# A fused state-space and feed-forward block with its gradients: channel order, one pass of magnitudes, split gates and a pipeline of state sums

## The chip, the cores and the metric

The kernel runs on one core of one Trainium2 chip. The metric is the device time of one execution in microseconds. A core has TensorE (PE, with its weight loads shown apart as PEld), VectorE (DVE), ScalarE (ACT), GpSimd (POOL) and SyncE (SP), and 16 DMA engines. Here nearly all transfers are issued by SP, in order.

## What is computed

For `x` of 2048 tokens by 512 channels the reference normalizes `x` to `xn`, runs a state-space convolution with 128 complex states per channel (`s`), runs a feed-forward net on the same `xn`, gates the one with the other, and returns the output and the gradients of all inputs but `B_x`, twelve arrays of bf16.

```python
P = jnp.exp(logdA[:, :, None] * l[None, None, :])
K = jnp.einsum("dn,dnl,dn->dl", Cc, P, dB).real
...
Yf = Uf * Kf[None, :, :, :]
y = irfft2(Yf, ...) + u * Dskip
...
h = silu(x @ w1);  out = h @ w2
...
xn = _layernorm(x); s = _A_ref(xn, ...); g = silu(_B_ref(xn, w1, w2))
return x + s * g
```

## The kernel before

The 512 channels are four blocks `b` of 128. Within a block a channel has two indexes, `q` (32) and `a` (4). The state-space part keeps its tables in the order (q, a); the channels of `xn`, `ds` and the outputs are in natural order, and strided access patterns lead from one to the other.

**Setup.** `layer_norm` (L223) makes `xn` from four chunks of `x`, `make_consts` (L108) the DFT matrices (`TF` by a sine on ACT, L142), `ssm_params` (L320) the rates `lamr` and `tau` and the weights `CT`.

**Forward.** `gen_ffn_fwd` (L481) is 8 chunks of 256 tokens: transposed `xn`, 56 matmuls a chunk with `W1` (L495), casts of `hT` on ACT, SiLU (L500), matmuls with `W2` (L507), stores to `Hd` and `Od`. Interleaved with it runs a chain over the blocks: `gen_tables` (L347) and `gen_conv_fwd` (L453). The tables need magnitudes `mag`, 31 exponentials of `lamr` (L356), and phases (sine, L376); their products are `E` and `Y`, stored to `Ed` and `Yd`; matmuls with `Y` (L408) and `SEL` (L419) give the convolution kernel, stored to `Kd`. `gen_conv_fwd` takes the spectrum `U` of `xn` and `KX` of the kernel (`dft_fwd`, L252, with a transposing DMA `dB` between two matmul stages), multiplies them (`cplx_mul`, L295), and goes back with `dft_inv` (L275), whose last matmuls (L291) write PSUM in natural channel order through a strided pattern.

**Gates.** For each block in turn `gen_gate_ds` (L515) loads the feed-forward result `Od` and the incoming gradient, makes `g` by SiLU and `ds`, stored to `dSd`; `gen_gate` (L529) loads `s` from `Sd` and `x`, writes the first output and `do`, the gradient that enters the feed-forward net. `g` has one buffer.

**Backward.** `gen_ffn_da` (L698) makes `dh` (L721, L723) and the gradient of `xn` (L732) for 8 chunks. Beside it a chain runs `gen_conv_bwd` (L547), which takes the spectrum of `ds` and gives the gradients of the kernel (`dKd`) and of `xn` (`dUd`), and `gen_ssm_bwd` (L585) for each block. That folds `dK` (L609), makes `Gb` (L615), and then works through four groups of 8 `q`: `YT` by transposing DMAs from `Yd`, matmuls `ps_v` (L628) that write PSUM in a strided order, casts `Vb` on ACT, four products `T` with `E` on DVE (L636), and sums over the 21 exponents, 84 matmuls of 64 columns with an identity (L641), all tiles with a single buffer. After four groups the block's parameter gradients follow (L655 on). What is left of the chain runs beside `gen_dw2` (L739), `gen_ln_bwd` (L772) and `gen_dw1` (L754).

**Order.** The generators are interleaved by weights, which gives the order in which the program is written; a scheduler then orders the instructions of each engine by that order and by when their operands are expected. On the chip each engine and each DMA queue keeps that order.

Of the kernel before, what the change touches and what calls it, by code (L numbers as in the profile page):

```python
# [9 lines left out]
ALU = mybir.AluOpType  # L10
# [5 lines left out]
P = 128  # L16
# [62 lines left out]

def interleave_until(gens, weights, other):  # L80
# [13 lines left out]
def slope_less_one(nc, u, h):  # L94

    nc.scalar.activation(out=h, in_=h, func=ACT.Tanh, scale=0.5)
    nc.vector.tensor_scalar(out=h, in0=h, scalar1=-0.5, scalar2=0.5, op0=ALU.mult, op1=ALU.add)
    nc.vector.tensor_single_scalar(out=u, in_=u, scalar=-1.0, op=ALU.add)
    nc.vector.tensor_tensor(out=u, in0=u, in1=h, op=ALU.mult)
# [8 lines left out]
def make_consts(k, wp):  # L108
# [141 lines left out]
def dft_fwd(k, U, X, ev):  # L252
# [22 lines left out]
def dft_inv(k, Y, ev, consume, natural=True):  # L275
    nc, w8, pc = k.nc, k.dft, k.pc
    A2 = w8.tile([P, 2, 16, P], BF16, name="dA2", tag="w8")
    for g0 in range(0, 16, 4):
# [5 lines left out]
        ev(A2[:].rearrange("p c t (g e) -> p g (c t) e", e=8)[:, g0:g0 + 4], ps[:])  # L284
    for h in range(2):
        ps = pc.tile([P, 8, P], F32, name="ps_i1", tag="pc")
        for j in range(8):
            t = 8 * h + j
            o = ps[:, j].rearrange("p (q a) -> p a q", a=4) if natural else ps[:, j]
            for c in range(2):  # L290
                nc.tensor.matmul(out=o, lhsT=k.TI[:, 2 * t + c, :], rhs=A2[:, c, t, :], start=(c == 0), stop=(c == 1))  # L291
# [3 lines left out]
def cplx_mul(k, out, a, b, conj=False):  # L295
# [24 lines left out]
def ssm_params(k, wp):  # L320
    nc, tbl, D = k.nc, k.p1, k.D
    TT = nc.vector.tensor_tensor
    S = load_params(k, wp, 0, D)
    ldt = wp.tile([P, D], BF16, name="ldt")
    nc.scalar.dma_start(ldt[:], k.ins["A_log_dt"].unsqueeze(0).to_broadcast([P, D]))
    nc.scalar.activation(out=k.dt[:], in_=ldt[:], func=ACT.Exp)
# [609 lines left out]
```

## Time and profile before

| | us |
|---|---|
| runs shown: median (lowest to highest) | 884.84 (877.52 to 887.74) |
| the profiled execution, its own time | 882.32 |
| its span, first to last instruction | 880.5 |
| mean granted TensorE clock | 0.901 |

The stages, by the first and last instructions of their parts: setup until about 48 us, forward to 309 (the last `ps_k` matmuls), the last block's transform and the gates to 419 (the first `ps_da` matmul), then the backward stages to the end. In the slices below (40 equal slices of the span) a digit is the busy share of an engine in tenths, PEclk the granted clock in tenths.

```profile
PE   0567697989968733602579999999999678878987
DVE  6967778569368500874385885977957456543420
ACT  0597978889888342432466847646752477632311
PEclk9989699999989675655889999999999899988999
DMA  8626367386556469697757569869545999757573
```

The row of PE has a trough in slices 14 to 19, which is the stretch from 309 to 419 us, and the clock falls with it.

### The profile page before, as it was taken

Reading aid. Unit: us, or ns where it says so; the run is one execution under the profiler, and the core shown is the slowest. Engines: PE = TensorE matmul, PEld = TensorE weight load, DVE = VectorE, ACT = ScalarE, POOL = GpSimd, SP = SyncE. Lnnn points to the kernel's source line nnn. Section 1 sums busy time; section 2 is a strip of 40 time slices with the busy share of each in tenths; the row PEclk is TensorE's granted clock in tenths of the full one; section 3 lists DMA queues with packets and bytes.
Section 4 is the critical chain, followed back from the end, with each engine's and each line's share of the span. In section 5 each row is a group of like instructions: output and inputs, shape, how many; then the busy total and the mean of one; then the engine's idle time right before and its main releaser. Section 6 shows DMA issues by size and latency. Waiting matters only on the chain. (4 is left out here: it accounts for less than half of the span.)

```text
span 880.5 us, 14322 instructions
## 1 busy us (share of the span) xinstructions
PE 652.9 (74%) x5692; PEld 464.6 (53%) x5692; DVE 542.5 (62%) x1141; ACT 510.4 (58%) x753; POOL 10.8 (1%) x70
## 2 busy tenths in 40 slices
PE   0567697989968733602579999999999678878987
PEld 0444364756636521401356787766876344447866
DVE  6967778569368500874385885977957456543420
ACT  0597978889888342432466847646752477632311
POOL 2000000000000000000000000000000000000000
PEclk9989699999989675655889999999999899988999
DMA  8626367386556469697757569869545999757573
GB/s 245 149 86 162 140 193 212 90 237 186 142 179 206 135 179 253 173 253 178 194 158 207 159 197 233 187 160 253 113 125 145 200 244 249 184 130 148 122 179 84
DMA packets 300151, 155.61 MB, mean 177 GB/s; under 512 B 215858, under 2 KB 286772, under 8 KB 297012
## 3 DMA queue, kind: packets, MB, share of 16 engines
q1 hardware_dynamic: 299796, 154.44, 68.3%
q8 instruction: 44, 0.72, 0.3%
q10 hardware_dynamic: 288, 0.26, 0.1%
q14 instruction: 23, 0.19, 0.1%
HBM read 48.23 MB, written 60.30 MB: 123 GB/s over the span
## 5 line engine op out<-in xcount | busy, mean ns | idle before, releaser
L495 PE MATMUL ps_h<-XT,W 128*128 128x256 bf16 x448 | 61.6, 285 | 38.1 <-DMA XT<-xn 28.4
L270 PE MATMUL ps_s<-dB,F 128*128 128x512 bf16 x96 | 40.4, 420 | 43.5 <-DMA dB<-dA 37.0
L495 PEld LDWEIGHTS <-W 128*128 128x128 bf16 x448 | 44.5, 103 | 49.8 <-issue 25.1
L636 DVE TENSOR_TENSOR T<-Vb,Eb 128x1344 bf16<-128x1344 bf16 x64 | 51.0, 852 | 30.3 <-ACT Vb L41 30.3
L41 ACT CAST Vb<-ps_v 128x672 bf16<-128x672 f32 x64 | 44.3, 719 | 40.1 <-PE ps_v L628 34.3
L41 ACT CAST dA<-ps_i 128x1024 bf16<-128x1024 f32 x48 | 46.6, 1018 | 34.7 <-PE ps_i L282 30.5
L260 PEld LDWEIGHTS <-TF 128*128 128x128 bf16 x384 | 37.4, 112 | 54.9 <-DMA ds_b<-dSd 36.5
L747 PE MATMUL ps_w<-do,a_tok 128*128 128x512 bf16 x224 | 54.6, 403 | 15.5 <-ACT a_tok L744 15.5
L507 PE MATMUL ps_o<-W,aT 128*128 128x512 bf16 x224 | 56.5, 394 | 11.5 <-ACT hT L41 8.4
L721 PE MATMUL ps_da<-doT,W2T 128*128 128x256 bf16 x448 | 59.3, 279 | 3.0 <-DVE dhT L723 2.4
L765 PE MATMUL ps_w<-dh_tok,xn 128*128 128x256 bf16 x448 | 56.0, 284 | 6.1 <-DMA dh_tok<-DHd 6.1
L41 ACT CAST dA<-ps_s 128x1024 bf16<-128x1024 f32 x48 | 46.8, 1021 | 23.2 <-PE ps_s L260 23.1
L41 ACT CAST o<-ps_w 128x256 bf16<-128x256 f32 (+1 forms) x42 | 18.5, 440 | 68.5 <-PE ps_w L765 59.3
L732 PE MATMUL ps_dx<-W1T,dhT 128*128 128x512 bf16 x224 | 56.7, 382 | 0.1
L628 PE MATMUL ps_v<-Gb,YT 128*128 128x168 bf16 x256 | 47.4, 357 | 10.9 <-DMA YT<-Yd 6.0
L721 PEld LDWEIGHTS <-W2T 128*128 128x128 bf16 x448 | 45.6, 103 | 13.0 <-issue 4.9
L765 PEld LDWEIGHTS <-xn 128*128 128x128 bf16 x448 | 45.4, 103 | 13.3 <-DMA dh_tok<-DHd 3.9
L641 PE MATMUL psS<-T,ident 128*128 128x64 bf16 x1008 | 42.3, 201 | 5.9 <-DVE T L636 5.7
L747 PEld LDWEIGHTS <-a_tok 128*128 128x128 bf16 x224 | 22.2, 103 | 45.6 <-ACT a_tok L744 18.6
L408 PE MATMUL ps_k<-W,Y 128*128 128x84 bf16 x512 | 33.6, 218 | 15.9 <-DVE Y L395 9.3
L641 PEld LDWEIGHTS <-ident 128*128 128x128 bf16 x1008 | 40.1, 100 | 9.5 <-issue 7.7
L723 DVE SCALAR_TENSOR_TENSOR dhT<-dhT,ps_da 128x512 bf16<-128x512 bf16 x56 | 37.4, 682 | 11.2 <-PE ps_da L721 10.8
(220 smaller groups left out, 1384.3 us busy)
## 6 DMA issues: line engine op xcount, KB each, us to landing
Yd<-Y SPq DMA_DIRECT2D x8, 1024.0 KB, 5.6
Hd<-hT SPq DMA_DIRECT2D x8, 896.0 KB, 6.0
Ed<-E SPq DMA_DIRECT2D x8, 672.0 KB, 3.0
Eb<-Ed SPq DMA_DIRECT2D x8, 672.0 KB, 5.4
Ud<-U SPq DMA_DIRECT2D x4, 1024.0 KB, 4.9
KXd<-KX SPq DMA_DIRECT2D x4, 1024.0 KB, 6.0
slope<-Hd SPq DMA_DIRECT2D x8, 512.0 KB, 5.2
sp_in<-Ud SPq DMA_DIRECT2D x4, 1024.0 KB, 5.4
```

Source lines behind the costliest of these rows:

```text
L41: return self.nc.scalar.copy(out=out, in_=in_)
L260: nc.tensor.matmul(out=ps[:, j], lhsT=k.TF[:, 8 * h + j, c, :], rhs=U(8 * h + j), start=True, stop=True)
L270: nc.tensor.matmul(out=ps[:, 4 * u:4 * u + 4], lhsT=F2[:, m0], rhs=B[:, 0, g0:g0 + 4, :], start=True, stop=False)
L495: nc.tensor.matmul(out=ps[:, j], lhsT=k.W1[:, dk, ft * P:ft * P + P], rhs=XTv[:, :, dk, :], start=(dk == 0), stop=(dk == DK - 1))
L507: nc.tensor.matmul(out=ps[:], lhsT=aT[:, ft, t * P:t * P + P], rhs=k.W2[:, ft, :], start=(ft == 0), stop=(ft == FT - 1))
L628: nc.tensor.matmul(out=ps[:, u, 168 * c:168 * c + 168].rearrange("p (w e a) -> p w a e", w=2, a=4), lhsT=YT[:, c, q + u, :], rhs=Gb[:, q0 ...
L636: TT(out=Tt[:, :, c].rearrange("p q w e a -> p q w (e a)"), in0=Vb[:, :, c], in1=Eq[:, ec].unsqueeze(2).to_broadcast([P, 8, 2, NE * 4]), o ...
L641: nc.tensor.matmul(out=psS[:, r], lhsT=ms[c][:], rhs=Tt[:, :, c, :, e, :], start=(c == 0 and e == 0), stop=(c == 1 and e == NE - 1))
L721: nc.tensor.matmul(out=ps[:, j], lhsT=W2T[:, dk, ft * P:ft * P + P], rhs=dTv[:, :, dk, :], start=(dk == 0), stop=(dk == DK - 1))
L732: nc.tensor.matmul(out=ps[:], lhsT=dhs[ft // 8][:, ft % 8, t * P:t * P + P], rhs=k.W1T[:, ft, :], start=(ft == 0), stop=(ft == FT - 1))
L747: nc.tensor.matmul(out=ps[:], lhsT=a[:, t, :], rhs=k.do[:, t, :], start=(t == 0), stop=(t == k.T - 1))
L765: nc.tensor.matmul(out=ps[:], lhsT=k.xn[:, t, dk * P:dk * P + P], rhs=dh[:, t].rearrange("p j n -> p (j n)"), start=(t == 0), stop=(t == k ...
```

## The change

It has six parts.

1. **Channel order.** `xn` and `ds` enter the DFT in natural order, read contiguously, and `dft_inv` writes contiguously. So that the tables agree, `lamr`, `tau` and `CT` are reordered once in setup, and the parameter gradients read the state sums through a strided pattern. `Gb` and `MK` take the order (exponent, a), so that `ps_v` is written contiguously.
2. **Magnitudes once.** `ssm_magnitudes` makes those of all four blocks with 31 activations of 512 columns in setup, stores them to a new DRAM tensor `Md`, and `gen_tables` loads its block's part. In setup the loads of `x` and of the parameters, the norm's chunks and the constants are written in another order.
3. **The chain of the forward stage.** The spectrum of `xn` is a generator of its own (`gen_conv_x`), run beside the tables of the same block; DFT generators yield between their stages. The forward stage ends with the feed-forward net; what is left of the chain runs after it, and the last block's `gen_conv_fwd` beside the gates.
4. **Gates split.** `gen_gate_pre` does all that needs no `s` (in halves of 8 token tiles): `g`, `ds` and the factor of `do`; `gate_post` multiplies by `s`. For block 3 it takes `s` straight from `dft_inv`. `gen_conv_bwd(0)` runs beside the other blocks' gates.
5. **Backward.** `gen_ffn_da` runs beside `gen_conv_bwd` of blocks 1 to 3 alone; all of `gen_ssm_bwd` runs in the last stage, beside dW2, dW1 and the norm's backward, as one pipeline over 16 groups, with two buffers for `YT`, `Vb`, the products and `Gb`, each group's sums written two groups late. The sums of the c = 0 products of both parts are taken in one matmul of 128 columns: 21 such and 42 of 64 columns a group.
6. **Queues.** Most stores go to POOL's queue (`k.st`), those of `Kd` and `dKd` to ACT's. `W2T` is loaded before the rest of the chain, `W1T` at the start of `gen_ffn_da`.

```diff
+    k.MK = const.tile([P, 2, NE, 4], BF16, name="MK")
...
-            o = ps[:, j].rearrange("p (q a) -> p a q", a=4) if natural else ps[:, j]
...
+                nc.tensor.matmul(out=ps[:, j], lhsT=k.TI[:, 2 * t + c, :], rhs=A2[:, c, t, :], start=(c == 0), stop=(c == 1))
...
+def ssm_magnitudes(k, wp, S, ldt):
+    nc, tbl, D = k.nc, k.p1, k.D
...
+    nc.vector.tensor_tensor(out=qa_out(lamr[:]), in0=qa_in(k.dt[:]), in1=qa_in(S["Ar"]), op=ALU.mult)
...
+    for i, e in enumerate(E_EXP + Y_EXP):
+        nc.scalar.activation(out=mag[:, :, i], in_=lamr[:].rearrange("p (b d) -> p b d", b=4), func=ACT.Exp, scale=float(e))
+    for b in range(4):
+        nc.sync.dma_start(k.Md[b], mag[:, b].rearrange("p e d -> p (e d)"))
...
-    for i, e in enumerate(E_EXP + Y_EXP):
-        last = nc.scalar.activation(out=mag[:, i], in_=k.lamr[:, bs], func=ACT.Exp, scale=float(e))
+    nc.sync.dma_start(mag[:].rearrange("p e d -> p (e d)"), k.Md[b])
...
-        nc.sync.dma_start(k.Kd[b, a].rearrange("i j r -> j i r"), KE[a:P:4].rearrange("p i t q -> p i (t q)"))
+        nc.scalar.dma_start(k.Kd[b, a].rearrange("i j r -> j i r"), KE[a:P:4].rearrange("p i t q -> p i (t q)"))
...
-    dft_fwd(k, lambda t: k.xn[:, t, bs].rearrange("p (q a) -> p a q", a=4), U, k.evc)
+    yield from dft_fwd(k, dft, lambda t: k.xn[:, t, bs], k.U, k.evc)
...
-        hT = fp.tile([P, FT, 256], BF16, name="hT", tag="hT", bufs=2)
+                hT = fp.tile([P, 8, 256], BF16, name="hT", tag="hT", bufs=3)
...
+                k.st(k.Hd[f0:f0 + n, :, cs].rearrange("f p n -> p f n"), hT[:, 0:n])
...
+def gen_gate_pre(k, b, pool):
...
+        n = dict(g=4, th=2, G=2, ds=1)
...
+        nc.scalar.activation(out=g[:], in_=th[:], func=ACT.Silu)
+        nc.scalar.activation(out=th[:], in_=th[:], func=ACT.Tanh, scale=0.5)
+        TT(out=ds[:], in0=G[:], in1=g[:], op=ALU.mult)
+        nc.sync.dma_start(k.dSd[b][:, cs], fl(ds))
...
+def gate_post(k, b, h, S, x=None):
...
+    TT(out=k.do[:, ts, bs], in0=k.do[:, ts, bs], in1=S, op=ALU.mult)
+    TT(out=g[:], in0=g[:], in1=S, op=ALU.mult)
+    TT(out=x[:], in0=x[:], in1=g[:], op=ALU.add)
+    k.st(k.o0_v[:, ts, bs], x[:])
+
+def gen_gate_post(k, b, pool):
+    for h in range(2):
+        S = pool.tile([P, 8, P], BF16, name="S", tag="S", bufs=1)
+        x = pool.tile([P, 8, P], BF16, name="x", tag="x", bufs=1)
...
-                        nc.tensor.matmul(out=ps[:, u, 168 * c:168 * c + 168].rearrange("p (w e a) -> p w a e", w=2, a=4), lhsT=YT[:, c, q + u, :],
-                                         rhs=Gb[:, q0 + q + u].rearrange("p (w a) e -> p w a e", w=2), start=True, stop=True)
+                nc.tensor.matmul(out=ps[:, u, 168 * c:168 * c + 168], lhsT=YT[:, c, q + u, :],
+                                 rhs=Gb[:, q0 + q + u].rearrange("p w x -> p (w x)"), start=True, stop=True)
...
+def ssm_sums(k, Tp, out):
...
+    for e in range(NE):
+        nc.tensor.matmul(out=psS[:].rearrange("p r q w a -> p (r q) w a"), lhsT=k.ident[:],
+                         rhs=Tp[:, :, :, 0, :, e, :].rearrange("p r q w a -> p (r q) w a"), start=(e == 0), stop=False)
+    for r, m in ((0, k.nident), (1, k.ident)):
+        for e in range(NE):
+            nc.tensor.matmul(out=psS[:, r], lhsT=m[:], rhs=Tp[:, r, :, 1, :, e, :], start=False, stop=(r == 1 and e == NE - 1))
+    nc.scalar.copy(out=out, in_=psS[:])
...
+    k.st = nc.gpsimd.dma_start
...
+            yield from woven([gen_tables(k, 0), gen_conv_x(k, 0)], [5, 1])
+            for b in range(1, 4):
+                yield from woven([gen_tables(k, b), chained([gen_conv_fwd(k, b - 1), gen_conv_x(k, b)])], [3, 2])
...
+        interleave_until([gen_ffn_fwd(k)], [1], ch)
...
+            nc.sync.dma_start_transpose(k.W2T[:], B_w2)
...
+            run(ch)
...
+            next(fwd3)
+            run(pre(3))
+            run(fwd3)
+            run(pre(0))
+            interleave([gen_conv_bwd(k, 0), chained([post(0), pre(1), post(1), pre(2), post(2)])], [1, 2])
...
+            interleave([chained(gen_conv_bwd(k, b) for b in range(1, 4)), gen_ffn_da(k, da)], [1, 2])
...
+        interleave([gen_ssm_bwd(k, sb), chained([gen_dw2(k, fw), gen_dw1(k, fw)]), after(8, gen_ln_bwd(k, fw))], [2, 1, 1])
```

454 lines of the change are left out of this document (260 added, 194 removed).

## The prediction

> **What bounds the kernel now.** I read the busy times of the page first, then the view by windows for the five stages that the code lays out, then in each stage the waits, the timeline and the groups by shape. The first rows give total busy time; the next ones give one stretch each, with the busy time of PE, PEld, DVE, ACT and POOL, then the granted clock, the DMA share and GB/s.
>
> ```profile
> PE 652.9 (74%) x5692; PEld 464.6 (53%) x5692; DVE 542.5 (62%) x1141; ACT 510.4 (58%) x753; POOL 10.8 (1%) x70
> DMA packets 300151, 155.61 MB, mean 177 GB/s; under 512 B 215858, under 2 KB 286772, under 8 KB 297012
> 0.00:48.00 48.00, 16.74 (x99) 11.02 (x100) 38.89 (x139) 17.51 (x18) 8.18 (x56) 1.00 0.78 200
> 48.00:309.00 261.00, 209.05 (x1687) 140.05 (x1686) 180.83 (x394) 215.82 (x391) 2.66 (x14) 0.91 0.55 162
> 309.00:419.00 110.00, 33.52 (x172) 21.45 (x171) 46.38 (x50) 34.59 (x38) 0.00 (x0) 0.62 0.84 208
> 419.00:880.50 461.50, 393.60 (x3738) 292.07 (x3737) 276.38 (x559) 242.52 (x308) 0.00 (x0) 0.95 0.72 175
> 678.00:782.00 104.00, 79.75 (x641) 45.11 (x638) 57.91 (x170) 65.32 (x93) 0.00 (x0) 0.93 0.91 212
> 678.00:880.50 202.50, 159.15 (x1508) 113.24 (x1505) 84.18 (x233) 89.62 (x141) 0.00 (x0) 0.92 0.75 169
> ```
>
> No one engine bounds the span; the limits change. Forward (48 to 309) has ACT busy 215.8 and PE 209 of 261 us. The gates (309 to 419) leave every engine mostly idle at a clock of 0.62 while DMA runs at 0.84. From 419 on PE is busy 393.6 of 461.5 us, so what is left there is PE work, with 67.9 us of idle time.
>
> **Setup and forward.** The magnitudes (L356) go from 124 activations of 128 columns inside the forward stage to 31 of 512 columns in setup, stored to `Md` and loaded once a block.
>
> ```profile
> L356 ACT ACTIVATE mag<-lamr 128x128 bf16<-128x128 f32 x124 | 27.6, 313 | 0.1
> 48.00:309.00 261.00, 32.88 (x129) 0.91 0.55 162
> ACT L142 <- DVE ks L141: 21.7, 1, 21.7
> 8.28 0.63 ACT L326 ACTIVATE dt<-ldt 128x512 bf16<-128x512 bf16 x1 [5.37 <-DMA ldt<-in_A_log_dt_dram]
> 12.64 1.36 DVE L247 TENSOR_SCALAR xn<-x_sb,rstd,nb 128x512 bf16<-128x512 bf16 x4
> 31.89 3.90 ACT L142 ACTIVATE TF<-ks,mpi 128x2048 bf16<-128x2048 int32 x2
> 28.43 5.28 PE L495 MATMUL ps_h<-XT,W 128*128 128x256 bf16 x24 [28.43 <-DMA XT<-xn]
> 317.86 2.57 SPq L443 DMA_DIRECT2D Kd<-KE  x4
> ```
>
> The second row is line 356 alone: 124 activations and 5 table loads, 32.9 us of ACT in forward. In setup ACT waits 21.7 us at L142. The new 31 take 31 x 0.63 = 19.5 us and can start once the first norm chunk is through (12.64 + 1.36 = 14.0) and `lamr` is made, so they end near 34 where the sine table began at 31.9: +3 us, between 0 and +6 (chunks two and three of `x` are now also queued on SP behind transposed parameters; PE started at 28.4 on that queue). The `Kd` stores move to ACT's queue: 2.57 us for each of three blocks inside the stage, on an engine with `hT` casts queued behind, which PE waits for; 0 to 7.7 us, taken in full. ACT then has 215.8 - 32.9 + 7.7 = 190.6 us.
>
> Matmul streams, from the timeline; the first pair is the inverse transform with strided and with contiguous output, the second the forward one with strided and contiguous input:
>
> ```profile
> 641.20 3.65 PE L291 MATMUL ps_i<-dA,TI 128*128 128x128 bf16 x32
> 450.96 1.95 PE L291 MATMUL ps_i<-dA,TI 128*128 128x128 bf16 x32 [1.16 <-ACT dA L41]
> 33.95 2.01 PE L260 MATMUL ps_s<-xn,TF 128*128 128x128 bf16 x16 [0.24 <-ACT TF L142]
> 128.30 1.06 PE L260 MATMUL ps_s<-Kb,TF 128*128 128x128 bf16 x16
> 654.61 1.17 PE L628 MATMUL ps_v<-Gb,YT 128*128 128x168 bf16 x7 [0.32 <-DMA YT<-Yd]
> 682.63 0.91 PE L641 MATMUL psS<-T,nident 128*128 128x64 bf16 x21
> 454.02 1.93 PE L282 MATMUL ps_i<-I,GX 128*128 128x256 bf16 x16 [0.25 <-ACT dD L567]
> ```
>
> A contiguous output saves (3.65 - 1.95) / 32 = 0.053 us a matmul, a contiguous input (2.01 - 1.06) / 16 = 0.059. In forward: 128 `xn` streams x 0.059 + 96 inverse ones x 0.053 = 12.7 us, so PE falls to 196.3 and is now the busier engine. If the busier one keeps its share of 0.83 (215.8 / 261), the stage takes 236.5: **-24.5 us**, between 0 (the chain of tables keeps its pace) and -33 (all of L356's time).
>
> [...]
>
> **Gates (309 to 419).**
>
> ```profile
> 323.25 9.15 SPq L880 DMA_TRANSPOSE W1T<-in_B_w_dram  x1
> 332.44 7.54 SPq L884 DMA_TRANSPOSE W2T<-in_B_w_dram  x1
> 346.87 0.61 PE L270 MATMUL ps_s<-dB,F 128*128 128x512 bf16 x1 [14.70 <-DMA dB<-dA]
> PE ps_s L260 <- DMA ds_b<-dSd: 35.1, 1, 35.1
> ACT g L523 <- DVE do L542: 20.9, 3, 7.9
> L538 DVE TENSOR_TENSOR sg<-S,g 128x2048 bf16<-128x2048 bf16 x4 | 4.9, 1222 | 28.5 <-DMA S<-Sd 28.5
> L98 DVE TENSOR_SCALAR dhT<-dhT 128x2048 bf16<-128x2048 bf16 x8 | 5.5, 686 | 14.2 <-ACT dhT L713 14.2
> x<-in_A_u_dram SPq DMA_DIRECT2D x4, 512.0 KB, 7.4
> out_dram<-x SPq DMA_DIRECT2D x4, 512.0 KB, 4.3
> 408.38 1.22 DVE L542 TENSOR_TENSOR do<-S,g 128x2048 bf16<-128x2048 bf16 x1
> 418.91 0.37 PE L721 MATMUL ps_da<-doT,W2T 128*128 128x256 bf16 x1 [0.32 <-DMA doT<-do]
> ```
>
> Now the last block's transform stands 14.7 us behind two weight transposes on SP; then four gates run in turn, each `g` waiting for the last `do`, and PE idles 35.1 us for `ds_b`. After, `pre` needs no state sum, so `dSd`, `ds_b` and `conv_bwd(0)` start while block 3 is still in its transform. What is late next is `post`: six halves with one `S` and one `x` buffer, so each is a load, an add and a store in turn: half of 7.4, 0.61 and half of 4.3, 6.5 us, up to 12.3 if a half costs a whole one's latency. Six take 39 to 74 us. They follow `pre` of block 0. That of blocks 3 and 0 is 2 x (3 x 1.22 + 3 x 0.69) = 11.5 us of DVE, and its loads stand in the same SP queue, so I let it end where that queue now clears, 346.9 (1.22 by L538's row, 0.69 by L98's). Last `do` then falls between 386 and 421, against 408.4. By the nearer row (half the bytes, half the landing) I take 386, and first `ps_da` as far behind it as now (418.9 - 408.4 = 10.5): 396.4, **-22.5 us**; -35 if `post` overlaps, +12 at the slow end. W1T's 9.15 us moves in front of the first `slope` loads of `gen_ffn_da`, covered by `conv_bwd(1)`; uncovered, it costs its 9.
>
> **From 419 on.** PE work that goes: `conv_bwd(0)` is already done (four groups of 16 at 1.93 and 3.65 + 1.95: 13.3); 256 `ps_v` with contiguous output, 0.053 scaled by 168/128 columns: 0.070 each, 17.8 (0 to half of the 1.17 / 7 shown, 21); the DFT of `ds` for three blocks 96 x 0.059 = 5.7, their inverse 96 x 0.053 = 5.1. In the state sums 42 matmuls of 64 columns become 21 of 128: 42 x 0.91 / 21 = 1.82 us against 21 at 0.061 (the contiguous row) to 0.087 (twice a short one): 0 to 0.54 a group; I take 0.25 x 16 = 4. Sum 45.9, PE 347.7.
>
> ```profile
> PE ps_w L747 <- ACT a_tok L744: 15.5, 8, 5.2
> L636 DVE TENSOR_TENSOR T<-Vb,Eb 128x1344 bf16<-128x1344 bf16 x64 | 51.0, 852 | 30.3 <-ACT Vb L41 30.3
> DMA packets 91817, 34.31 MB, mean 169 GB/s; under 512 B 77720, under 2 KB 88217, under 8 KB 91801
> YT<-Yd SPq DMA_TRANSPOSE x14, 4.3
> Eb<-Ed SPq DMA_DIRECT2D x3, 672.0 KB, 6.2
> ```
>
> Idle: the pipeline over 16 groups (two `Vb`, `Tp`, `YT`, `Gb`) and the merge with dW2, dW1 and the norm's backward give PE other work where it now waits 15.5 for `a_tok` and DVE 30.3 for `Vb`. I take a third of the 67.9 off, 45 left; ends 67.9 and 20. So 347.7 + 45 = 393: **-68.5 us** (-46 to -94). DMA checks it. The last three rows are the stretch from 678 alone. All of `gen_ssm_bwd` now falls into the last stage: 34.3 MB + 18 more YT x 0.26 + 5 Eb x 0.69 + 12 GE x 0.13 = 44 MB. At 169 / 0.75 = 225 GB/s for full load that needs 196 us, and 215 at the 0.91 share that was held for 104 us. DMA is next in line.
>
> **The sum**, against the profiled execution's own span: 880.5 + 3 - 24.5 - 22.5 - 68.5 = 768, and 1.8 around it (882.3 in all): **770 us**. That execution lies 0.3% under the median of 884.84.
>
> **Rivals.** The row is POOL's memsets of `Y`, which wait for PE.
>
> ```profile
> POOL Y L364 <- PE ps_k L408: 246.6, 7, 58.8
> ```
>
> 1. *DMA holds the last stage at the share it has now.* 44 MB at 169 GB/s is 260 us, against the 215 that my sum allows: 770 + 45 = 815. For it: share 0.75 with 34 MB, transposes all on SP. Against: 0.91 for 104 us.
> 2. *Other side.* The whole kernel stays at its mean rate: `Md` adds 2 x 4.06 MB, the last `Sd` leaves 1.05, so 162.7 MB at 177 GB/s is 919 + 2 = 921 us, slower. It decides where the mean rate stays under 162.7 / 884.84 = 184 GB/s. Against it: the stages held 208 and 212 when they had work queued, and forward runs at a share of 0.55.
> 3. *The idle time goes too*: all good ends, 880.5 - 33 - 35 - 94 + 1.8 = 720.
> 4. *`post` at its slow end and no better forward*: 770 + 22.5 + 12 + 24.5 = 829.
> 5. *Stores on POOL come late.* Buffers of dW2 and dW1 (two each) then hold back the 21 evictions. [...] In forward the `Hd` and `Od` stores queue behind the memsets of `Y` on POOL. I cost that at nothing, since three `hT` halves leave two halves' time, 2 x 261 / 16 = 33 us; a memset that waits its longest, 58.8, would hold `ps_h` for the rest, 26. [...]
>
> **How the numbers follow.** Chances: forecast with rival 5, 750 to 795, 0.47 (0.05 of it rival 5); rival 3 and what lies between, under 750, 0.25; rivals 1 and 4, 795 to 840, 0.16; more of the gain lost but still 1% faster 0.04; no change 0.03; rival 2, 0.05. A difference under 1% can't be told from none here. Faster 0.92, same 0.03, slower 0.05. The range leaves out the lowest tenth of rival 3 and the cases above rivals 1 and 4: 718 to 836, where the good ends (720) and the bad ends of all terms (880.5 + 6 + 12 - 46 + 1.8 = 854) nearly lie.
>
> **What would show it.** L356's row as 31 of about 0.6 us ending before 36 us; `ps_v` rows near half their time; first `ps_da` near 375 (396.4 + 3 - 24.5); the last stage's DMA share over 0.85 with PE idle under 45 us after that. Wrong if the forward stage keeps 261 us, if first `ps_da` still stands 110 us behind the last `ps_k`, or if the last stage takes over 240 us at a DMA share under 0.8.

## The result

| us | before | after |
|---|---|---|
| median (lowest to highest, runs) | 884.62 (877.52 to 887.74, 4) | 828.23 (822.57 to 832.47, 4) |
| the profiled execution: its own time, span | 882.32, 880.5 | 822.57, 820.7 |
| last `ps_k` (end of the tables) | 308 | 298.1 |
| first `ps_da` (end of the gates) | 418.9 | 377.9 |
| last `ps_dx` (start of the last stage) | 677 | 575.4 |

The ratio is 0.937 (95% interval 0.929 to 0.945): 56 us faster, half of the 115 that were forecast. The page after has these totals:

```profile
PE 606.2 (74%) x5356; PEld 419.0 (51%) x5356; DVE 545.3 (66%) x1163; ACT 490.3 (60%) x670; POOL 74.7 (9%) x163
DMA packets 272257, 162.65 MB, mean 198 GB/s; under 512 B 204992, under 2 KB 254144, under 8 KB 269120
```

And the view by windows, cut at the same marks as before (busy PE, PEld, DVE, ACT, POOL; granted clock; DMA share; GB/s):

```profile
48.00:298.00 250.00, 193.54 (x1641) 124.25 (x1641) 188.47 (x409) 172.76 (x250) 21.02 (x35) 0.90 0.69 201
298.00:378.00 80.00, 34.47 (x199) 19.09 (x197) 44.41 (x74) 35.31 (x47) 7.09 (x8) 0.68 0.87 215
378.00:575.40 197.40, 164.96 (x1333) 115.44 (x1331) 140.75 (x199) 123.38 (x125) 3.13 (x4) 0.97 0.69 187
575.40:778.80 203.40, 161.43 (x1766) 119.47 (x1767) 122.59 (x306) 115.52 (x177) 24.95 (x45) 0.90 0.93 196
778.80:820.70 41.90, 33.03 (x296) 27.87 (x294) 9.79 (x38) 7.76 (x20) 7.53 (x12) 0.97 0.51 112
378.00:820.70 442.70, 359.42 (x3393) 262.78 (x3391) 273.13 (x543) 246.66 (x322) 35.60 (x61) 0.94 0.78 184
```

The first two rows together come near what was hoped for: they end at 378, where 375 was forecast. The last row is the miss: from the first `ps_da` on, 461.5 us became 442.7 instead of 393. Where this time lies is read from the three rows above it, and from the same three stretches of the kernel before:

```profile
419.00:677.40 258.40, 233.85 (x2229) 178.25 (x2229) 192.17 (x326) 152.37 (x167) 0.00 (x0) 0.98 0.70 180
677.40:832.80 155.40, 120.41 (x1176) 81.15 (x1174) 75.31 (x196) 81.64 (x119) 0.00 (x0) 0.91 0.81 182
832.80:880.50 47.70, 39.33 (x338) 32.68 (x336) 8.90 (x39) 8.51 (x22) 0.00 (x0) 0.96 0.56 126
```

Until the last `ps_dx`, PE idles 32 of 197 us; before, it idled 25 of 258. From there to the last `psS` the state sums take 203 us, 42 of them idle on PE, with the DMA engines at 0.93; before, what was left of the sums took 155, with 35 idle. Behind them PE has little but dW1, for 42 us against 48 before, with 8 to 9 idle in both. The start of the last stage in PE's timeline, and two of SP's rows there:

```profile
574.78 0.59 PE L872 MATMUL ps_dx<-W1T,dhT 128*128 128x512 bf16 x2
586.73 0.59 PE L673 MATMUL G<-GE,zero 128*128 128x512 bf16 x1 [11.36 <-DMA GE<-dKd]
595.51 1.28 PE L707 MATMUL ps_v<-Gb,YT 128*128 128x168 bf16 x8 [2.38 <-DVE Gb L685]
600.30 1.04 PE L887 MATMUL ps_w<-do,a_tok 128*128 128x512 bf16 x2 [3.51 <-ACT a_tok L884]
```

```profile
577.37 1.26 SPq L327 DMA_TRANSPOSE par_Ci<-in_A_C_im_dram  x1
579.30 1.35 SPq L658 DMA_DIRECT2D GE<-dKd  x2
```

PE waits for `GE`, which SP asks for behind six transposed parameters; of the 298 transfers that SP issued in this execution, none landed before the one that it had asked for ahead of it. Before, the first blocks' state sums ran beside other work, and from 520 to 678 us PE was nearly full.

```profile
520.00:620.00 100.00, 94.31 (x871) 69.92 (x870) 77.18 (x139) 61.33 (x66) 0.00 (x0) 1.00 0.84 208
620.00:678.00 58.00, 56.66 (x617) 45.20 (x618) 46.42 (x93) 29.10 (x37) 0.00 (x0) 1.00 0.49 130
```

### The profile page after: what moved, and what is told of

It reads as the page before. It is cut to its first block, busy times and chain, and to the rows that moved or that the text cites. A ratio compares the mean times of both kernels' runs of the same rounds, so it can differ in the third digit from the quotient of the medians.

```text
span 820.7 us, 13722 instructions
## 1 busy us (share of the span) xinstructions
PE 606.2 (74%) x5356; PEld 419.0 (51%) x5356; DVE 545.3 (66%) x1163; ACT 490.3 (60%) x670; POOL 74.7 (9%) x163
## 5 line engine op out<-in xcount | busy, mean ns | idle before, releaser
L535 PE MATMUL ps_h<-XT,W 128*128 128x256 bf16 x448 | 59.9, 283 | 29.9 <-DMA XT<-xn 25.8
L282 PE MATMUL ps_s<-dB,F 128*128 128x512 bf16 x96 | 44.6, 465 | 47.9 <-DMA dB<-dA 47.5
L887 PE MATMUL ps_w<-do,a_tok 128*128 128x512 bf16 x224 | 58.7, 408 | 15.6 <-ACT a_tok L884 15.6
L717 DVE TENSOR_TENSOR Tp<-Vb,Eb 128x1344 bf16<-128x1344 bf16 x64 | 52.5, 853 | 22.7 <-issue 9.2
L535 PEld LDWEIGHTS <-W 128*128 128x128 bf16 x448 | 43.5, 101 | 40.4 <-issue 19.6
L42 ACT CAST dA<-ps_s 128x1024 bf16<-128x1024 f32 x48 | 46.0, 1019 | 28.5 <-PE ps_s L270 28.4
L861 PE MATMUL ps_da<-doT,W2T 128*128 128x256 bf16 x448 | 55.1, 273 | 2.2 <-DVE dhT L863 2.1
L905 PE MATMUL ps_w<-dh_tok,xn 128*128 128x256 bf16 x448 | 52.6, 273 | 2.2 <-DMA dh_tok<-DHd 2.2
L872 PE MATMUL ps_dx<-W1T,dhT 128*128 128x512 bf16 x224 | 51.8, 379 | 1.0 <-DVE dhT L863 1.0
L431 DVE TENSOR_TENSOR W<-E,CT 128x672 bf16<-128x672 bf16 x64 | 29.4, 503 | 33.0 <-DMA Kd<-KE 19.4
L270 PEld LDWEIGHTS <-TF 128*128 128x128 bf16 x384 | 27.6, 107 | 38.8 <-DMA Kb<-Kd 18.7
L863 DVE SCALAR_TENSOR_TENSOR dhT<-dhT,ps_da 128x512 bf16<-128x512 bf16 x56 | 36.6, 684 | 15.9 <-PE ps_da L861 15.6
L884 ACT ACTIVATE a_tok<-a_tok 128x2048 bf16<-128x2048 bf16 x14 | 26.7, 1910 | 33.1 <-DMA a_tok<-Hd 33.1
L283 PE MATMUL ps_s<-dB,F 128*128 128x512 bf16 x96 | 44.1, 460 | 0.0
L436 PE MATMUL ps_k<-W,Y 128*128 128x84 bf16 x512 | 30.6, 206 | 17.8 <-DVE W L431 10.4
L404 ACT ACTIVATE sn<-V,pi 128x1024 bf16<-128x1024 int32 (+3 forms) x40 | 37.9, 967 | 9.5 <-DVE V L402 9.3
```

The source lines that it names most:

```text
L42: return self.nc.scalar.copy(out=out, in_=in_)
L282: nc.tensor.matmul(out=ps[:, 4 * u:4 * u + 4], lhsT=F2[:, m0], rhs=B[:, 0, g0:g0 + 4, :], start=True, stop=False)
L283: nc.tensor.matmul(out=ps[:, 4 * u:4 * u + 4], lhsT=F2[:, m1], rhs=B[:, 1, g0:g0 + 4, :], start=False, stop=True)
L404: nc.scalar.activation(out=sn[:, :, 0:n], in_=V[:, :, 0:n], func=ACT.Sin, scale=-2 * math.pi / PH, bias=k.pi[:])
L535: nc.tensor.matmul(out=ps[:, j], lhsT=k.W1[:, dk, ft * P:ft * P + P], rhs=XTv[:, :, dk, :], start=(dk == 0), stop=(dk == DK - 1))
L717: k.nc.vector.tensor_tensor(out=Tp[:, r, :, c].rearrange("p q w e a -> p q w (e a)"), in0=Vb[:, :, c], in1=Eq[:, ec].unsqueeze(2).to_broad ...
```

## The experiments

Each is one edit of the changed kernel; what a text calls theory A, B, C and so on, it explains where the letter first stands (A to D: the last stage is held by its transfers, by its start, by stores on POOL that come late, or the stage before lost its filler). "Sums" is the time from the last `ps_dx` to the last `psS`, with the DMA share and PE's busy time in it; "tail" is what follows. All but the median are from the profiled execution; that of the changed kernel was the fastest of its four, 5.7 us under their median, so differences of its marks can fall short of differences of medians. Medians that differ by under 5 us are taken as equal, since the changed kernel's own runs spread over 10.

| run | median | last ps_k | last ps_dx | sums | DMA | PE | tail |
|---|---|---|---|---|---|---|---|
| changed | 828.2 | 298.1 | 575.4 | 203.4 | 0.93 | 161 | 41.9 |
| mags_per_block | 851.9 | 336.5 | 610.2 | 199.1 | 0.93 | 160 | 42.3 |
| stores_sp | 815.8 | 287.4 | 566.4 | 207.5 | 0.88 | 164 | 40.2 |
| memset_dve | 819.3 | 292.8 | 571.9 | 202.7 | 0.94 | 165 | 41.0 |
| streams_strided | 854.1 | 303.7 | 601.0 | 210.3 | 0.90 | 179 | 41.3 |
| par_late | 825.4 | 296.1 | 575.4 | 203.6 | 0.95 | 160 | 43.4 |
| ln_late | 829.1 | 295.5 | 575.4 | 209.4 | 0.91 | 163 | 44.3 |
| atok_ahead | 827.7 | 300.8 | 580.5 | 203.0 | 0.93 | 161 | 41.5 |
| yt_half | 815.9 | 302.0 | 581.7 | 191.9 | 0.81 | 155 | 41.3 |
| yt_plain | 813.5 | 302.3 | 579.1 | 195.8 | 0.83 | 157 | 41.4 |
| yt_early | 820.4 | 313.2 | 585.7 | 191.4 | 0.82 | 155 | 41.4 |
| plain_off_sp | 845.3 | 300.7 | 580.0 | 221.2 | 0.85 | 164 | 42.3 |
| sums_in_turn | 832.6 | 298.2 | 577.5 | 209.0 | 0.92 | 164 | 41.2 |
| no_dw | 756.6 | 298.2 | 578.1 | 158.2 | 0.69 | 100 | 18.5 |
| no_ln | 818.9 | 295.2 | 575.1 | 188.3 | 0.81 | 157 | 45.6 |
| dw2_half | 817.5 | 298.9 | 599.6 | 196.3 | 0.96 | 158 | 19.6 |
| combo1 | 807.4 | 285.5 | 586.6 | 198.8 | 0.94 | 158 | 21.0 |
| combo2 | 810.0 | 295.0 | 602.8 | 181.6 | 0.91 | 155 | 19.3 |
| combo3 | 809.5 | 288.0 | 593.4 | 194.1 | 0.92 | 151 | 18.5 |

### Forward: magnitudes and POOL's order

```diff
-    nc.sync.dma_start(mag[:].rearrange("p e d -> p (e d)"), k.Md[b])
+    nc.sync.dma_start(lamr[:], k.Md[b])
+    for i, e in enumerate(E_EXP + Y_EXP):
+        nc.scalar.activation(out=mag[:, i], in_=lamr[:], func=ACT.Exp, scale=float(e))
```

> The magnitudes are made block by block in the forward stage again, 31 activations of 128 columns each, from a small table kept in DRAM; the rest is as changed. The prediction's row gives 32.9 us more of ACT in forward, and setup loses 31 activations of 512 columns. If ACT sets the forward stage (215.8 of 261 us before): forward grows by 15 to 25 us, 840 to 852. If the chain of tables, PE (193.5 of 250 us) or POOL's order sets it: 0 to 10 us, and setup gives 0 to 3 back: 825 to 837.

851.85, 23.6 us more. Its row of magnitudes, and beside it the setup row of the changed kernel:

```profile
L384 ACT ACTIVATE mag<-lamr_b 128x128 bf16<-128x128 f32 x124 | 27.8, 304 | 5.0 <-issue 4.9
```

```profile
L353 ACT ACTIVATE mag_all<-lamr 128x512 bf16<-128x512 f32 x31 | 16.2, 616 | 2.8 <-DVE lamr L348 2.8
```

So making the magnitudes once is worth about 24 us in the whole and 38 at the last `ps_k`, as much as was forecast for the whole stage. But ACT is busy 0.69 of the forward stage with the magnitudes made once and 0.79 with them made block by block, and PE 0.77 and 0.69, so neither engine's sum alone holds the tables; that the exponentials stood in ACT's order ahead of casts and sines is the likely reason, not shown.

```diff
-    k.st = nc.gpsimd.dma_start
+    k.st = nc.sync.dma_start
```

> All stores that the change put on POOL's queue go back to SP's. Theory C (stores on POOL late): landing goes back from 4.7 to about 2.9 us, buffers come free earlier: 812 to 824. Theories A, B and D: POOL's stores move 18.1 MB at 7.5% of the engines' time and nothing waits for them; on SP they stand in one queue with the loads and each waits there for its eviction, so loads behind it come late: 830 to 850.

815.8, in theory C's band. 10.6 us are gone at the last `ps_k`, none in the last stage. The first `ps_da` comes even 27 us earlier, at 350.7, but the stage that it opens grows by 18, so that 9 are left at the last `ps_dx`. What on POOL was late, its waits in the forward stage of the changed kernel show (total, times, longest):

```profile
POOL Hd L542 <- ACT hT L42: 79.9, 10, 18.9
POOL Y L392 <- PE ps_k L436: 49.8, 6, 22.4
```

Stores and the memsets of `Y` stand in one order, each behind the other's wait.

```diff
-        nc.gpsimd.memset(Y[:, 0, :, 0, :], 1.0)
-        nc.gpsimd.memset(Y[:, 1, :, 0, :], 0.0)
+        nc.vector.memset(Y[:, 0, :, 0, :], 1.0)
+        nc.vector.memset(Y[:, 1, :, 0, :], 0.0)
```

> Stores stay on POOL's queue; the memsets of Y in the tables move from POOL to DVE, 16 of 64 columns, under 2 us in all. With all stores on SP the forward stage (last ps_k) ended at 287.4 instead of 298.1 and the whole at 815.8 instead of 828.2. Theory C1 (order on POOL): a memset of Y stood behind Hd and Od stores that waited for ACT, and DVE's tables behind the memset: the 10.6 us come back here too, last ps_k near 288, 815 to 820. Theory C2 (software descriptors land late, 4.7 against 2.9 us, and hold buffers): nothing changes, 825 to 832.

819.3 with all stores still on POOL: 8.9 of the 12.4 us come back, and the other 3.5 are within the spread. But the direction was not quite C1's. The last `ps_o` of the feed-forward net comes at 231 instead of 246, the last `ps_k` only 5 earlier: the stores that stood behind a memset held the net more than the memsets held the tables. So the order on POOL explains most of the 12.4 us.

### Contiguous streams

The first stage of the transform of x and ds, `ps_i` (L303) and `ps_v` now read and write with a step of four. This is more than undoing the change: before, these matmuls had the step on one side only, and a third of the `ps_i` had none. Of `ps_v`:

```diff
-                nc.tensor.matmul(out=ps[:, u, 168 * c:168 * c + 168], lhsT=YT[:, c, q + u, :],
-                                 rhs=Gb[:, q0 + q + u].rearrange("p w x -> p (w x)"), start=True, stop=True)
+                nc.tensor.matmul(out=ps[:, u, 168 * c:168 * c + 168].rearrange("p (w e a) -> p w a e", w=2, a=4), lhsT=YT[:, c, q + u, :],
+                                 rhs=Gb[:, q0 + q + u].rearrange("p w (e a) -> p w a e", a=4), start=True, stop=True)
```

> Same result, but the matmuls that the change made contiguous read and write with a step of four again: the forward transform of x and ds, the inverse transform's last step, ps_v. By the prediction's rows PE gains 12.7 us in forward, 10.8 + 2.8 in the backward transforms and 17.8 in the state sums, 44 in all. If PE sets the pace of every stage the whole is 860 to 875. Theory A: the last stage is held by transfers and orders, its 17.8 us vanish in PE's idle time there (51 us), and the whole is 838 to 856.

854.1, 26 us more. By windows PE's busy time grows by 8.6 us in forward, 21.9 beside `gen_conv_bwd` and 17.7 in the last stage, and these stages grow by 5.7, 19.2 and 6.3. A microsecond of PE is thus worth 0.9 beside `gen_conv_bwd` and 0.36 in the last stage, as theory A expects: PE alone doesn't set that stage.

### The last stage: single waits

```diff
-    par = load_params(k, sb, 0, k.D)
-    par["dt"] = k.dt[:]
...
+            if i == 1:
+                par = load_params(k, sb, 0, k.D)
+                par["dt"] = k.dt[:]
```

> Changed kernel 828.2 us; the six transposed parameters of the state sums are loaded after the second group's YT instead of first, so GE and the first YT stand first in SP's queue. Theory A (transfers): the last stage is as long as its transfers allow (DMA share 0.85 over all of it, 1.03 from 616 to 748, and 0.83 even in the hole at its start), so GE comes some 10 us earlier, first ps_v near 586 instead of 595.5, and the end does not move: within 3 us of 828. Theory B (start): the last stage loses its time in the hole, PE busy 6.1 of 25 us: 816 to 820. Theory C (stores on POOL late) and theory D (the stage before has lost its filler): no change.

825.4. First `ps_v` at 584.1 instead of 595.5, last `psS` at 779.0 instead of 778.8: the 11 us that the start gave are lost again behind it. Theory B falls.

```diff
+    def load(ft):
+        a = fw.tile([P, k.T, P], BF16, name="a_tok", tag="a_tok", bufs=3)
...
+    nxt = load(fts[0])
+    for ft in fts:
+        a, nxt = nxt, load(ft + 1) if ft < fts[-1] else None
```

> dW2's a_tok is loaded one tile ahead, in three buffers instead of two. Theory E (order on ACT): in the last stage ACT stood 33.1 us before a Silu whose a_tok had just been asked for, with evictions of Vb and Sa queued behind it; that wait falls under 12 us, PE's 15.6 us for a_tok under 6, and the whole is 812 to 820. Theory A (transfers): no transfer becomes smaller, the waits move to YT, Eb or dh_tok: within 4 us of 828.

827.7. PE's wait for `a_tok` falls from 15.6 to 3.6 us as theory E said, and nothing comes of it: theory E falls, and A's expectation is met.

```diff
-        interleave([gen_ssm_bwd(k, sb), chained([gen_dw2(k, fw), gen_dw1(k, fw)]), after(8, gen_ln_bwd(k, fw))], [2, 1, 1])
+        interleave([gen_ssm_bwd(k, sb), chained([gen_dw2(k, fw), gen_dw1(k, fw)]), after(26, gen_ln_bwd(k, fw))], [2, 1, 1])
```

> The norm's backward pass starts after 26 rounds of the last stage instead of 8, when the state sums are nearly through. Its 8 x 4 transfers of 256 KB are 8.4 MB. Theory A (transfers): they take 8.4 / 220 = 38 us of the saturated stretch and now fall where the DMA share was 0.50 to 0.55 (748 to 820): state sums end 25 to 38 us earlier and the whole is 803 to 815 us. Theory B (start), C (stores) and D (filler before): the saturated stretch was not what held the stage, PE was: within 3 us of 828, or later if the norm's backward now ends last.

829.1, but this tells little. The scheduler, which orders by due times, took the norm's loads up again: SP asked for the first at 663 us instead of 636, still amid the sums.

```profile
635.81 0.62 SPq L918 DMA_DIRECT2D du<-dUd  x1
```

```profile
663.30 0.58 SPq L918 DMA_DIRECT2D du<-dUd  x1
```

### The last stage: transfers, chain, sharing

```diff
-    YT = sb.tile([P, 2, 8, P], BF16, name="YT", tag="YT", bufs=2)
+    if q0:
+        return k.YT
+    YT = k.YT = sb.tile([P, 2, 8, P], BF16, name="YT", tag="YT", bufs=2)
```

> Of the state sums' YT only the first eight columns of each half are loaded and used for the second eight too: 16 of the 32 transposes, 4.2 MB, are left out. Theory A (transfers): 4.2 MB at 220 GB/s is 19 us less in the saturated stretch: 809 to 818, and the DMA share from 616 on stays near 1 until the sums end. Theory B, C and D: a single late load at the start is not touched, within 4 us of 828.

815.9. The sums take 191.9 instead of 203.4 us, as theory A has it. But the DMA share falls to 0.81, where theory A had it stay near 1 from 616 us on, so something else then holds them.

```diff
-        k.nc.sync.dma_start_transpose(YT[:, c], k.Yd[b, h][:, (c * 16 + q0) * P:(c * 16 + q0 + 8) * P])
+        k.nc.sync.dma_start(YT[:, c].rearrange("p q j -> p (q j)"), k.Yd[b, h][:, (c * 16 + q0) * P:(c * 16 + q0 + 8) * P])
```

> Y's tables are loaded for the state sums by plain transfers of the same bytes into the same buffers; their transposition is left out, so ps_v multiplies the table's other side. Theory A1 (bytes): 44.7 MB stay 44.7 MB, within 4 us of 828. Theory A2 (transposes): leaving out 4.2 MB of them took the 16 engines' busy time in the last stage from 0.85 x 245.3 = 208.5 to 0.76 x 233.2 = 177 us, 7.5 us a MB, while the gates' stage moves 17.2 MB, nearly all plain, in 70 us, 4 us a MB; 8.4 MB made plain take 8.4 x 3.5 = 29 us of busy time away: 800 to 816. Theory D (order on PE, ACT and DVE alone): within 4 us of 828.

813.5 at the same bytes: A1 and D fall, A2's band is met. Busy transfer time in the sums falls from 0.93 x 203.4 = 189 to 0.83 x 195.8 = 163 us, 26 where 29 were expected; 8 of them come off the sums.

```diff
-        nc.sync.dma_start(k.Yd[b, h], Y[:].rearrange("p c q j a -> p (c q j a)"))
+        for c in range(2):
+            YT = tbl.tile([P, 16, P], BF16, name="YT", tag="YT")
+            nc.sync.dma_start_transpose(YT[:], Y[:, c].rearrange("p q j a -> p (q j a)"))
+            nc.sync.dma_start(k.Yd[b, h][:, 2048 * c:2048 * c + 2048], YT[:].rearrange("p q k -> p (q k)"))
```

> Same result: Y's tables are transposed when they are made, in the forward stage (DMA share 0.69, 250 us), stored so, and loaded plain in the last stage. Theory A2: 63 us of busy transfer time move to a stage with 77 us to spare, 15 to 30 us come off the last stage, forward grows by 0 to 8 us: 803 to 818. Against it: the transforms' own transposes (dB, 8 us to landing) stand in the same queue in forward, and PE waits for them; if each of the 8 is late by a table's 7 us, forward grows by 20 or more: 826 to 840.

820.4. The last stage is 232.8 us instead of 245.3, and forward ends 15 us later: the gain and the "against it" both came, and 8 us are left by the medians.

SP's issue was the next suspect. In the changed kernel two transposed loads of `YT` held SP's queue for 3.17 us, the next two for 5.02, and a plain load of `Eb` between them for 0.52:

```profile
583.34 3.17 SPq L696 DMA_TRANSPOSE YT<-Yd  x2
586.62 0.52 SPq L689 DMA_DIRECT2D Eb<-Ed  x1
587.19 5.02 SPq L696 DMA_TRANSPOSE YT<-Yd  x2
592.26 2.85 SPq L883 DMA_TRANSPOSE a_tok<-Hd  x1
```

```diff
-    k.nc.sync.dma_start(E[:].rearrange("p c q e a -> p (c q e a)"), k.Ed[b, h])
+    k.nc.scalar.dma_start(E[:].rearrange("p c q e a -> p (c q e a)"), k.Ed[b, h])
...
-        nc.sync.dma_start(Gt[:], k.g_v[:, 2 * c:2 * c + 2, :])
+        nc.gpsimd.dma_start(Gt[:], k.g_v[:, 2 * c:2 * c + 2, :])
```

> All plain loads of the last stage leave SP: GE and Eb are asked for on ACT's queue, du, Gt and pd on POOL's; the transposes stay on SP. From 575 to 764 SP issues for about 160 of 189 us: YT 1.85 us each, a_tok 3.3, dh_tok 3.1, the plain ones 0.45 to 0.7, 26 us in all. Theory S (SP's issue is the bound of that stretch): the sums come 12 to 25 us earlier, 806 to 818. Theory P: SP was late with nothing that PE had no other work for: 824 to 832.

845.3, 17 us more and outside both bands. On POOL's queue the norm's loads stood behind stores that wait for evictions (waits of this run):

```profile
POOL out_dram L890 <- ACT o L42: 82.4, 11, 21.4
POOL du L918 <- DVE pd_l L928: 30.0, 4, 16.2
POOL du L918 <- DMA GE<-dKd: 27.1, 1, 27.1
```

The edit put new waits in place of what it removed, so it can't price SP's issue. yt_plain bounds it: 32 loads take 0.43 us each of SP's queue instead of 1.80, 44 us less issue in all, for 8 us of the sums. Issue and transfer time fall together there, as in yt_half and yt_early, so these runs don't tell which of the two gave the 8 to 12 us.

The pipeline itself was undone in the order of the program:

```diff
+        vb = ssm_v(k, q0, Gb, ssm_turned(k, b, h, q0, sb), sb)
+        yield
+        tp = ssm_products(k, q0, vb, E, sb)
+        yield
+        ssm_sums(k, tp, S[:, :, 16 * h + q0:16 * h + q0 + 8])
+        yield
```

> The state sums' pipeline is undone in the order of the program: each group's YT, ps_v, products and sums follow each other as before the change, the fold of a block stands at its start; buffers, merging and all else stay. The prediction gave the pipeline and the merging a third of 67.9 us of idle PE. Theory K: the order of the chain sets the stage, 840 to 865. Theory P: PE, transfers and queue set it and dW fills the gaps whichever way: 824 to 836.

832.6, in theory P's band: 4 us, inside the spread of the runs. With double buffers and the scheduler's own order the written order brings little.

```diff
-        interleave([gen_ssm_bwd(k, sb), chained([gen_dw2(k, fw), gen_dw1(k, fw)]), after(8, gen_ln_bwd(k, fw))], [2, 1, 1])
+        interleave([gen_ssm_bwd(k, sb), after(1, iter(())), after(8, gen_ln_bwd(k, fw))], [2, 1, 1])
```

> dW2 and dW1 are left out; the last stage is the state sums and the norm's backward pass alone. In every run so far the sums, from the last ps_dx to the last psS, took 191 to 210 us with some 160 us of PE work in them, of which dW2 and dW1 are about half. Theory P (the sums share PE, transfers and queue with dW; nothing of their own holds them): 90 to 130 us. Theory K (their own chain of fold, Gb, YT, ps_v, Vb, Tp, psS holds them, dW only fills it): over 170 us, and then all dW work behind them is tail.

756.6; the sums take 158.2 us, between the two theories' bounds. With only the norm's backward pass beside them, DVE is nearly full for half of that time:

```profile
640.00:720.00 80.00, 49.13 (x688) 44.00 (x685) 76.90 (x214) 48.14 (x90) 11.30 (x21) 0.77 0.69 172
```

DVE has 76.9 of 80 us there. Over the whole 158.2 us it has 121 (0.77), and with dW beside the sums 123 of 203 (0.60).

```diff
-        interleave([gen_ssm_bwd(k, sb), chained([gen_dw2(k, fw), gen_dw1(k, fw)]), after(8, gen_ln_bwd(k, fw))], [2, 1, 1])
+        interleave([gen_ssm_bwd(k, sb), chained([gen_dw2(k, fw), gen_dw1(k, fw)])], [2, 1])
```

> The norm's backward pass is left out: no PE work, but 38 us of DVE, 26 us of ACT and 8.4 MB of plain transfers go from the last stage. Theory V (the sums' own work on DVE holds the stage, with the norm's beside it: without dW the sums took 158 us and DVE was 0.96 busy from 640 to 720): the sums end 20 to 35 us earlier, but dW's PE work then fills less of them and moves behind: 805 to 818. Theory P (PE's 194 us and the start's hole set the end whatever stands beside them): within 5 us of 828.

818.9, just above theory V's band: the sums end 15 us earlier instead of 20 to 35, and 4 of it go into the tail. The edit took 31 us of DVE's busy time away and 36 of transfer time (0.93 x 203.4 against 0.81 x 188.3 is 189 against 153), so it doesn't tell which counted.

### Moving work, and candidates

```diff
+            interleave([chained(gen_conv_bwd(k, b) for b in range(1, 4)), gen_ffn_da(k, da), paced(gen_dw2(k, da, range(7)), 6, 4)], [1, 2, 1])
...
+        interleave([gen_ssm_bwd(k, sb), chained([gen_dw2(k, fw, range(7, k.FT)), gen_dw1(k, fw)]), after(8, gen_ln_bwd(k, fw))], [2, 1, 1])
```

> As the kernel that loads a_tok ahead, and seven of dW2's fourteen tiles are made beside the stage of ps_da instead of in the last one: 7 x 16 matmuls of 512 columns at 0.22 us, 24.6 us of PE and 3.7 MB. Theory D (that stage lost its filler): its 32 us of idle PE take most of this, it grows by under 10 us, the last stage shrinks by 17 to 25: 8 to 18 us under the kernel that only loads ahead. Theory A gives the same sign, 3.7 MB / 220 GB/s = 17 us less at the end against a stage with a DMA share of 0.69. Theory F (that stage is bound by its own order of work on PE, ACT and DVE): it grows by as much as the last one shrinks, within 4 us of the kernel that only loads ahead.

817.5, 10.2 under atok_ahead, in the band of D, but not by its mechanism. The stage of `ps_da`, by windows, with the added tiles:

```profile
377.80:599.60 221.80, 190.24 (x1445) 125.95 (x1443) 141.31 (x199) 139.40 (x139) 7.04 (x11) 0.98 0.72 188
```

It grows from 200.6 to 221.8 us, and PE idles 31.6 of them as it did 32.0 in atok_ahead: the filler filled nothing, which is theory F's mechanism. The gain is in the last stage, whose sums take 196.3 us instead of 203.0 and whose tail falls from 41.5 to 19.6: it shrinks by 28.6 for a growth of 21.2.

Then combinations: stores on SP until the last stage opens,

```diff
+        k.st = nc.gpsimd.dma_start
         sb = pool("sb", es=es_2)
```

with the edits of atok_ahead and dw2_half (combo1), with those of yt_early and par_late besides (combo2), and combo1 with ten tiles (combo3).

> A candidate: stores on SP up to the last stage and on POOL in it, a_tok loaded one tile ahead, seven of dW2's tiles beside ps_da. If the two gains (12.4 us in forward and gates, 10.2 us in the last two stages) lie in different stages and add: 803 to 809. If the forward gain only moves the same transfers into each other: 812 to 818.

807.4, ratio 0.915 (0.912 to 0.919): the two gains add, and this version beats both kernels.

> A candidate: the 807.4 us kernel (stores on SP up to the last stage, a_tok ahead, seven dW2 tiles beside ps_da) with Y's tables transposed in the forward stage and the parameters loaded late. If the 7.8 us of the early transposition add: 797 to 802. If stores and transposes on SP's one queue delay the forward stage: 806 to 816.

810.0: the shortest sums of all, 181.6 us, and a forward stage 9.5 us longer, with gates of 82 us instead of 63, where SP's one queue now has stores and transposes.

> A candidate: as the 807.4 us kernel with ten of dW2's tiles beside ps_da instead of seven. Its tail of dW1 behind the last psS was 14.5 us; three tiles are 3 x 3.5 = 10.6 us of PE. By the price shown (24.6 us of PE added there lengthened that stage by 21.3 and shortened the last by 28.7): 3 us less, 802 to 808. If the added tiles fill no idle time and the sums do not shrink: 808 to 813.

809.5 (ratio 0.918, 0.914 to 0.921): no gain over combo1. Three more tiles lengthened the stage of `ps_da` by 4 us, and sums and tail became 7 us shorter; the tables ended 2.5 us later.

## Why the prediction was right and wrong

- **Setup, +3.** It went the other way: first PE work at 25.8 us instead of 28.4. The 31 activations took 16.2 us where 19.5 were reckoned, and ran from 9.3 to 25.5 us instead of from 14 to 34.
- **Forward, -24.5.** The last `ps_k` moved by 10 us, not 21.5. PE's busy time came out as reckoned (193.5 us for 196.3), and the edit of the magnitudes has the worth that it was given (mags_per_block). But the busier engine did not keep its share of 0.83: PE is at 0.77. (With 0.83 unrounded the sum itself gives 237.4 instead of 236.5.) The stores behind memsets on POOL, which rival 5 cost at nothing, took 9 to 12 us of the whole; with them on SP the last `ps_k` stands at 287.4, where 309 + 3 - 24.5 = 287.5 was forecast.
- **Gates, -22.5.** 110 us became 80, -30, between the value taken and the good end. Two errors cancel inside it: the six halves of `post` came 10.5 us apart (their `do` on DVE from 303.1 to 355.8) instead of 6.5, but began 22 us before the time taken for them, 346.9 - 21.5 = 325.4. And that the first `ps_da` stands at 377.9, where 375 was forecast, is luck too: 10.6 us were missed at the last `ps_k` and 7.5 gained behind it.
- **From 419 on, PE work -45.9.** It fell by 34.2. The rows of before and after for the terms:

```profile
L628 PE MATMUL ps_v<-Gb,YT 128*128 128x168 bf16 x256 | 47.4, 357 | 10.9 <-DMA YT<-Yd 6.0 <-DVE Gb L615 4.3 <-ACT dD L567 0.4
L641 PE MATMUL psS<-T,ident 128*128 128x64 bf16 x1008 | 42.3, 201 | 5.9 <-DVE T L636 5.7
L641 PE MATMUL psS<-T,nident 128*128 128x64 bf16 x336 | 15.5, 203 | 0.1
L282 PE MATMUL ps_i<-I,KGX 128*128 128x256 bf16 x128 | 18.0, 292 | 9.8 <-DVE KGX L305 7.2 <-ACT Vb L41 1.6 <-ACT dA L41 0.9
L260 PE MATMUL ps_s<-ds_b,TF 128*128 128x128 bf16 x96 | 12.5, 292 | 0.6 <-DMA ds_b<-dSd 0.6
```

```profile
L707 PE MATMUL ps_v<-Gb,YT 128*128 128x168 bf16 x256 | 29.5, 252 | 10.0 <-ACT Vb L42 7.2 <-DVE Gb L685 2.4
L726 PE MATMUL psS<-Tp,ident 128*128 128x128 bf16 x336 | 29.5, 238 | 1.8 <-DVE ddt L788 1.8
L730 PE MATMUL psS<-Tp,nident 128*128 128x64 bf16 x336 | 15.0, 201 | 0.0
L730 PE MATMUL psS<-Tp,ident 128*128 128x64 bf16 x336 | 14.7, 201 | 0.0
L294 PE MATMUL ps_i<-I,KGX 128*128 128x256 bf16 x128 | 18.4, 292 | 7.3 <-DVE KGX L317 6.5 <-ACT dA L42 0.6
L270 PE MATMUL ps_s<-ds_b,TF 128*128 128x128 bf16 x96 | 6.8, 219 | 4.4 <-DMA ds_b<-dSd 4.3
```

  `ps_v` gave 17.9 (17.8 forecast), the transform of `ds` 5.7 (5.7), its inverse 6.8 (5.1; L291's row had 22.4 us, L303's 15.6). The sums gave nothing: 57.8 us before, 59.2 after, with 0.088 a merged matmul, the bound of twice a short one. And `conv_bwd(0)`, 13.3, didn't leave: the x128 of the `KGX` rows are four blocks of 32 in both, so its way back still runs behind the first `ps_da`. The other 5 us of the 34.2 lie in rows that the change leaves as they were.
- **From 419 on, idle 67.9 to 45: the step that failed**, "PE other work where it now waits ... a third of the 67.9 off". Idle time rose to 83.3, which is 38 of the 50 us that are missing behind the first `ps_da`. No stretch gave any back: 25 us became 32 until the last `ps_dx`, 35 became 42 until the last `psS`, and 8 became 9 in the tail. Of the two waits that the step names, DVE's for `Vb` fell from 30.3 to 9.2 us, but PE's for `a_tok` stayed at 15.6, and new ones came at the start and before `ps_v` (waits of the last stage, then DVE's row):

```profile
PE ps_w L887 <- ACT a_tok L884: 15.6, 6, 3.7
PE G L673 <- DMA GE<-dKd: 11.4, 1, 11.4
PE ps_v L707 <- ACT Vb L42: 7.2, 4, 5.0
```

```profile
L717 DVE TENSOR_TENSOR Tp<-Vb,Eb 128x1344 bf16<-128x1344 bf16 x64 | 52.5, 853 | 22.7 <-issue 9.2 <-ACT Vb L42 9.2 <-PE psS L730 4.2
```

  Nor would their removal have been enough: atok_ahead took 12 us off PE's wait for `a_tok` and par_late 11 off the start, and neither changed the time. The merge put all state sums into one stage where transfers are at 0.93, PE at 0.79 and DVE at 0.60. It also took them away from `gen_conv_bwd`, beside which PE had been busy 151 of 158 us. That their leaving made the idle time there is not shown: the one run that put other work in their place, dw2_half, left it as it was.
- **DMA next in line** was right and sized low: 44.6 MB came, in 0.85 x 245.3 = 209 us of busy time against 196, since transposes cost more than their bytes (in yt_plain the same bytes, loaded plain, took 26 us less of it). But "215 at the 0.91 share" took the share as even; it was 0.93 for 203 us and 0.51 for 42. The sign "over 0.85 with PE idle under 45 us" came by half: 0.85, with 83.3 idle.
- **Rivals.** Rival 1 named the last stage's transfers; the stage took 245 us, not 260, and the runs put 8 to 12 us of it to transfers or their issue. That the result lies between its 815 and rival 4's 829 is luck: `post` was not slow, and the gates gave more than was taken. Rival 2 was excluded by 198 GB/s.

What sets the last stage is shown only in part. With the transfers' busy time cut by 26 to 34 us, and SP's issue with it, the sums take 191 to 196 us, 8 to 12 less. There the DMA engines are at 0.81 to 0.83 and PE at 0.80 to 0.81, so neither is full. Which of PE's order, ACT, DVE and SP's queue holds the rest stays open, and with it the cause of most of the 38 us of idle time.

## What to carry to other kernels

Before stages are merged, add up each resource over the merged stage, transposes at their own rate (here 26 us of busy time more than plain loads of the same 8.4 MB, by yt_plain), and don't book a wait as filled because it has got a neighbour: here every stretch kept its idle time. In the last stage a single wait that was removed came back elsewhere (par_late, atok_ahead), and moving a whole piece of work to another stage paid (dw2_half, 10 us), though it filled no idle time there. An engine's queue that gets a new kind of work (stores on POOL, 9 to 12 us of the whole here) must be read for what already waits in it.

## What was not expected of the hardware

- In the changed kernel a transposing load held SP's queue for 1.2 to 3.9 us per 256 KB `YT`, 1.80 in the mean of 32, and 3.3 in the mean for a 512 KB `a_tok`; plain loads of 256 to 672 KB (`du`, `Eb`) for about 0.5.
- Strided reading and writing did not add up here: with both, in streams_strided, `ps_i` took 46.4 us for 384 matmuls, 0.121 each, against 0.114 with the strided output alone before (3.65 / 32) and 0.061 with neither (1.95 / 32). The step in the input alone cost as much, 0.059: the `ds` rows above, alike but for that step, have 0.130 us a matmul against 0.071.

```profile
L305 PE MATMUL ps_i<-dA,TI 128*128 128x128 bf16 x384 | 46.4, 296 | 9.3 <-ACT dA L42 9.1
```
